# One-core S5 scan and dilated attention: wider products, two copied key rows, a shorter weighted sum, and powers and reloads on ScalarE

## The chip, the cores and the metric

The kernel runs on one core of one Trainium2 chip. The time is the device time of one execution, as the median of several runs. TensorE (PE) multiplies matrices into PSUM, VectorE (DVE) and ScalarE (ACT) work on tiles of 128 partitions, GpSimd (POOL) makes constants and SyncE (SP) issues most of the transfers. Data that is too large for one tile step lives in SBUF; the results of matmuls lie in PSUM banks and have to be evicted by DVE or ACT before a bank is used again.

## The reference: what is computed

Two independent layers act on inputs of 2048 positions by 448 features, in bf16, and their outputs stand side by side.

```python
# A: a diagonal state-space layer, 448 complex states
Lam_bar = exp(dt * Lam);  B_bar = ((Lam_bar - 1) / Lam)[:, None] * Bmat
h[t] = Lam_bar * h[t-1] + (x @ B_bar.T)[t]
y = 2 * real(h @ Cmat.T) + x * Dskip
# B: dilated sliding attention, 16 heads of 28, 8 taps, step 2
logits[s, w] = q[s] . k[s - 2 w] * 28**-0.5      (masked where s - 2w < 0)
o[s] = sum_w softmax(logits)[s, w] * v[s - 2 w]
out = concat(y, o @ wo)
```

## The kernel before, in words

The 2048 positions are laid out as 128 columns (position blocks) of 16 rows j. So a shift by two positions is a shift by two rows of a tile, and only where it runs past the first row does it become a shift by one column.

**Layer B.** PE projects q and k into PSUM banks `qk_ps`; ACT (L215, L217) and DVE (L219, L221) evict them into the tile `qk`. For half of the queries at a time (b = 1, then b = 0), DVE multiplies q with k row by row for two of the eight taps in one instruction, into the tile `prods` (L651, L653, L657). Shifts that run past row 0 need other rows and a column offset, so such a product is cut into several instructions. A ring of three buffers of 4096 columns holds products. PE sums the products over the head's dimensions into `logits` (L669, L675), with 32 columns of the array per matmul, and adds the mask (L287). DVE takes the maximum (`mx`, L698), PE subtracts it, ACT takes the exponential (L708), PE sums, DVE normalizes (L717, L719) and SP transposes the result into `attn`. Meanwhile PE projects v into banks `v_ps` (L750 opens a bank, L757 fills it) and ACT evicts them into `vd`. The weighted sum is made four times, for four groups g of queries. In each, four multiplications of 3584 columns (L814) alternate with three additions (L817), and one addition of 1792 columns joins the halves (L826; in two parts for the last group, L829). The result is transposed and multiplied with `wo` (L864, L888, L895).

**Layer A.** The 448 states are seven blocks m. For each of them DVE makes the matrices of powers `pw` as one product of 128x1920 (L1177). Input terms are summed by PE into banks `scp`, `scb`, `scP` (L1227, L1236), and a chain of short matmuls with ACT evictions between them carries the state over the columns (L1246 to L1287). Sixteen times a state is put back into a bank by a matmul with the identity (L1303, L1317). `y_ps` collects the output with `Ccat`, and a part with `Dg` (made by ACT, L1132).

**What sets the order.** A list of unit numbers, `ORDER`, is run by a planner, which appends each unit's instructions to its engine. A unit that may go to ACT or DVE stands there with 1000 added for its second engine. Each engine then runs its own list in order, and a semaphore makes it wait for what another engine has to deliver. There are six banks `s` and one two-bank buffer `W` of PSUM. A `v_ps` matmul that opens a bank waits until ACT or DVE has evicted what was in it before.

Of the kernel before, what the change touches and what calls it, by code (L numbers as in the profile page):

```python
# [96 lines left out]
def vec2(n):  # L97
    return n / 1920.0 + 0.07
# [107 lines left out]
class Ctx:  # L206
# [111 lines left out]
class PartB:  # L318
# [262 lines left out]
    def qk(self, b, prio):  # L581
# [8 lines left out]
        for g in (2 * b + 1, 2 * b):  # L590
            par = g - 2 * b
            j0 = 4 * g
            for tp in (3, 2, 1, 0):
# [967 lines left out]
```

## Time and profile before

| | |
|---|---|
| median of 3 runs | 139.11 us (138.9 to 139.13) |
| profiled execution, span | 136.8 us |
| PE busy | 131.0 us (96%), 1066 matmuls |
| DVE busy | 123.1 us (90%), 134 instructions |
| ACT busy | 88.3 us (65%), 199 instructions |
| granted TensorE clock | 1.00 in all stretches |

The span is from the first to the last recorded instruction. The page gives the profiled execution no other time than that span; what the runs measure is 2.3 us more. A busy share counts instructions from start to end, and on one engine a next one can begin before the last has ended; so the distance from one start to the next is the price of an instruction in a row of them, and it is less than its duration.

### The profile page before, as it was taken

What the parts mean: (1) busy time and instruction counts of PE and PEld (TensorE: products, weight loads), DVE (VectorE), ACT (ScalarE), POOL (GpSimd) and SP (SyncE); (2) the same over time, 40 slices, a digit from 0 to 9 for tenths busy, and PEclk for the clock granted to TensorE, in tenths of its full rate; (3) what the DMA queues carried; (4) which work ended last, traced back from release to release, by engine and by line L of the source; (5) the groups of instructions that cost most, each with busy time, mean ns of one, the idle gap of its engine ahead of it and who ended that gap; (6) DMA issues with size and microseconds to landing.
All of it is one profiled execution on the core that took longest, in us unless ns stands there. A gap on an engine that the chain in (4) does not pass through costs nothing.

```text
span 136.8 us, 2838 instructions
## 1 busy us (share of the span) xinstructions
PE 131.0 (96%) x1066; PEld 67.2 (49%) x1071; DVE 123.1 (90%) x134; ACT 88.3 (65%) x199; POOL 17.5 (13%) x69
## 2 busy tenths in 40 slices
PE   7999999999999999999999999999999999999890
PEld 2534335444455453656444564556665545545450
DVE  1379998999999999997999999999999999999950
ACT  3455588998554976757795998779546461433561
POOL 7489830025000000000000000000000000000000
PEclk9999999999999999999999999999999999999999
DMA  4968943647555524667999029460074425744263
GB/s 130 271 128 204 187 87 59 156 117 112 84 113 53 99 50 108 172 119 113 195 218 203 0 41 233 133 143 3 0 61 109 138 65 146 160 136 134 74 194 101
DMA packets 41694, 16.58 MB, mean 121 GB/s; under 512 B 33685, under 2 KB 41044, under 8 KB 41681
## 3 DMA queue, kind: packets, MB, share of 16 engines
q1 hardware_dynamic: 41618, 16.40, 54.8%
q8 instruction: 8, 0.13, 0.4%
q14 instruction: 5, 0.04, 0.1%
q10 hardware_dynamic: 63, 0.01, 0.0%
HBM read 4.32 MB, written 3.67 MB: 58 GB/s over the span
## 4 chain that ended last, share of the span: by engine, by line
DVE 39%; PE 38%; SPq 10%; issue 5%; ACT 3%; DMA 2%; DVEq 0%; ACTq 0%
DVE rb L817 12%; DVE prods L814 11%; SPq L363 7%; PE v_ps L757 6%; PE scb L1227 5%; DVE rb L814 4%; PE scp L1227 4%; PE logits L669 3%; DVE pw L1177 2%; DMA rb<-in_B_x_dram 2%; PE qk_ps L478 2%; DVE prods L653 2%; PE wo_ps L895 2%; DVE rb L826 2%; ACT qk L215 1%
## 5 line engine op out<-in xcount | busy, mean ns | idle before, releaser
L814 DVE TENSOR_TENSOR prods<-attn,vd 128x3584 bf16<-128x3584 bf16 x12 | 24.0, 2016 | 0.0
L817 DVE TENSOR_TENSOR rb<-rb,prods 128x3584 bf16<-128x3584 bf16 x11 | 22.2, 2018 | 0.1
L653 DVE TENSOR_TENSOR prods<-qk 128x3072 bf16<-128x3072 bf16 (+1 forms) x15 | 19.1, 1324 | 0.0
L215 ACT CAST qk<-wo_ps 128x448 bf16<-128x448 f32 (+1 forms) x16 | 8.2, 527 | 10.0 <-PE wo_ps L888 7.8
L478 PE MATMUL qk_ps<-rb 128*128 128x512 bf16 x60 | 14.4, 379 | 0.3 <-DMA rb<-in_B_x_dram 0.3
L1424 PE MATMUL y_ps<-Ccat,qk 128*128 128x448 bf16 x60 | 14.6, 352 | 0.0
L215 ACT CAST vd<-v_ps 128x448 bf16<-128x448 f32 x16 | 7.9, 540 | 5.2 <-PE v_ps L757 4.9
L1227 PEld LDWEIGHTS <-Bcat 128*128 128x128 bf16 x84 | 7.5, 100 | 7.4 <-issue 1.1
L1274 ACT CAST ubuf<-scb 128x64 bf16<-128x64 f32 x35 | 7.3, 220 | 5.9 <-PE scb L1281 3.5
L1424 PE MATMUL y_ps<-Ccat,h 128*128 128x448 bf16 x45 | 11.0, 353 | 0.0
L1227 PE MATMUL scb<-xaT_sb,Bcat 128*128 128x512 bf16 x42 | 10.9, 380 | 0.0
L757 PE MATMUL v_ps<-rb 128*128 128x448 bf16 x48 | 10.1, 353 | 0.0
L217 ACT ACTIVATE qk<-qk_ps 64x512 bf16<-64x512 f32 (+1 forms) x15 | 8.9, 599 | 1.5 <-PE qk_ps L485 1.0
L478 PEld LDWEIGHTS <-rb 128*128 128x128 bf16 x60 | 5.6, 97 | 7.4 <-issue 0.7
L657 DVE TENSOR_TENSOR prods<-qk 128x768 bf16<-128x768 bf16 (+3 forms) x18 | 9.1, 565 | 0.1
L1424 PEld LDWEIGHTS <-qk 128*128 128x128 bf16 x60 | 5.9, 98 | 5.4
L814 DVE TENSOR_TENSOR rb<-attn,vd 128x3584 bf16<-128x3584 bf16 x4 | 8.1, 2020 | 0.1
L888 PE MATMUL wo_ps<-wo_p,rb 128*128 128x448 bf16 x36 | 8.1, 353 | 0.0
L1177 DVE TENSOR_TENSOR pw<-Dm,spair 128x1920 bf16<-128x1920 bf16 x7 | 8.0, 1150 | 0.0
L1227 PE MATMUL scp<-xaT_sb,Bcat 128*128 128x512 bf16 x30 | 7.8, 381 | 0.0
L215 ACT CAST qk<-qk_ps 128x512 bf16<-128x512 f32 (+2 forms) x11 | 6.3, 585 | 2.3 <-PE qk_ps L485 1.1
L215 ACT CAST qk<-y_ps 128x448 bf16<-128x448 f32 (+1 forms) x9 | 5.6, 662 | 3.1 <-PE y_ps L1424 3.1
(197 smaller groups left out, 258.9 us busy)
## 6 DMA issues: line engine op xcount, KB each, us to landing
out_dram<-qk SPq DMA_DIRECT2D x32, 112.0 KB, 1.7
vd<-vd SPq DMA_DIRECT2D x3, 392.0 KB, 4.4
rb<-in_B_wqkv_dram SPq DMA_DIRECT2D x3, 336.0 KB, 4.4
qk<-in_A_x_dram SPq DMA_DIRECT2D x1, 448.0 KB
ra<-in_A_B_re_dram SPq DMA_DIRECT2D x1, 392.0 KB, 4.2
ra<-in_A_B_im_dram SPq DMA_DIRECT2D x1, 392.0 KB
rb<-in_A_C_re_dram SPq DMA_DIRECT2D x4, 98.0 KB, 2.9
rb<-in_A_C_im_dram SPq DMA_DIRECT2D x4, 98.0 KB, 3.9
```

Source lines behind the costliest of these rows:

```text
L215: nc.scalar.copy(out, in_)
L217: nc.scalar.mul(out, in_, scale)
L363: nc.sync.dma_start(self.xT[:, j], bass.AP(x.tensor, x.offset + j * D - DT, [[T * D, NCH], [1, KT * NCH]]), transpose=True)
L478: nc.tensor.matmul(out(n), lhsT=w(n, full, k), rhs=self.xT[:, j:j + 4, k, :], start=(not rfirst and k == 1), stop=(rfirst and k == KT - 1) ...
L653: V.tensor_tensor(out.rearrange("p i j k q -> p i (j k) q"), qq.unsqueeze(1).to_broadcast([NCH, 2, 4 * nk, NCH]), bass.AP(kk.tensor, kk.of ...
L657: V.tensor_tensor(jk(out[:, i, a:e]), qq, kk, op=ALU.mult)
L757: nc.tensor.matmul(box["ps"][:].rearrange("p h d -> p (h d)"), lhsT=self.xT[:, j, k, :], rhs=self.wv[:, k, :], start=False, stop=(k == KT ...
L814: V.tensor_tensor(tmp[i].rearrange("p (j d h) -> p j d h", j=8, d=DH), aa, self.vd[:, o:o + 8], op=ALU.mult)
L817: V.tensor_tensor(acc, acc, tmp[i], op=ALU.add)
L1177: V.tensor_tensor(t[:], self.o["Dm"][:].rearrange("p (a b) -> p a b", b=2).unsqueeze(1).to_broadcast([NCH, 2 * NPW, 32, 2]), self.sp[:, m ...
L1227: mt(box[i], lhsT=self.Bcat[:, k, m, :], rhs=self.xk(slice(i, None, 4), k), start=(i % 2 == 0 and k == 0), stop=False, **kw)
L1424: nc.tensor.matmul(ps, lhsT=h, rhs=self.Ccat[:, m, :], start=(m == 0 and not skip), stop=(m == NM - 1), skip_group_check=True)
```

## The change

1. **Products of up to four taps.** Two rows are kept ahead of row 0 in the key tiles, copies of the last two rows shifted by one column (`u_halo`, `u_halo3`). Products of q and k are cut by half of the taps and no longer by two: 6144 columns where four taps have one form, 3072 or 1536 otherwise. The products of the remaining 64 feature rows have their own buffer of 2048 columns, and the ring has two buffers of 6144. The sums on PE take 512 columns a matmul, not 256.
2. **Weighted sum.** The eight products of a group lie side by side in the space of the ring: two multiplications of 3584 columns and one of 7168, then one addition of 7168, one of 3584 and one of 1792 columns (the last group: two parts of the last).
3. **Powers on ACT.** A unit `powers` may go to ACT: 30 instructions of 64 columns with a scale from a tile of 128 x 1. `ORDER` sends one of the seven there (1257). One more POOL instruction makes the scale tile.
4. **Reloads on ACT.** A state that is put back into a bank can be a copy by ACT. `ORDER` sends five of the sixteen there.
5. **A new `ORDER`** for all units; some setup tiles are used again in place.

The core of the diff:

```diff
+        self.u_halo = cx.double(768, self.kTh[:, 0:KH, :, 2:QW], self.kT[:, T - KH:T, :, 0:NCH], [self.u_pad[1], *self.u_k[3]], 0)
+        self.u_halo3 = cx.double(256, self.k3h[:, 0:KH, 2:QW], self.k3[:, T - KH:T, 0:NCH], [...], 0)
...
+                        out = ub["pr"][:, p0:p0 + np_].rearrange("p i j k q -> p i (j k) q")
+                        qq = jk(q[:, j0:j0 + 4]).unsqueeze(1).to_broadcast([NCH, np_, 4 * nk, NCH])
+                        kk = jk(kh[:, KH + o:KH + o + 4, :, c:c + NCH])
+                        V.tensor_tensor(out, qq, bass.AP(kk.tensor, kk.offset, [kk.ap[0], [DIL * nk * QW, np_], *kk.ap[1:]]), op=ALU.mult)
...
+                            nc.tensor.matmul(at(h, i), lhsT=z, rhs=pr[:, :, i, k, :].rearrange("p (a b) q -> p a b q", a=2),
...
-                    def add(i):
-                        V.tensor_tensor(acc, acc, tmp[i], op=ALU.add)
...
+            def fold(n, out=None, pb=pb):
+                V.tensor_tensor(pb[:, 0:n] if out is None else out, pb[:, 0:n], pb[:, n:2 * n], op=ALU.add)
...
+            for u0, nu in ((5, 1), (4, 1), (0, 2)):
...
+            if eng == "ACT":
+                for k in range(NPW):
+                    for h in range(2):
+                        nc.scalar.activation(t[:, 2 * k + h].rearrange("p a b -> p (a b)"), self.o["Dm"][:], ACT.Copy,
+                                             scale=self.sp32[:, h, m * NPW + k:m * NPW + k + 1])
...
+            def reload(eng, out, in_):
+                if eng == "ACT":
+                    nc.scalar.copy(out, in_)
+                else:
+                    mt(out, lhsT=cx.ident[:], rhs=in_, start=True, stop=False, **kw)
...
+    0, 4, 21, 22, 2, 3, 1, 5, 6, 37, 39, 38, 24, 41, 9, 26, 42, 1040, 28, 29, 50, 8, 51, 45, 1043, 63, 46, 30, 7,
...
+    136, 494, 188, 182, 1257, 186, 138, 485, 495, 507, 143, 512, 513, 515, 131, 180, 514, 144, 524, 508, 516, 510,
```

Three places show how the instructions move. The first is ACT between the last evictions of q and k (`qk_ps`) and the exponential of the softmax of b = 1 (`ex_sb`). Before:

```order
L217 ACTIVATE qk<-qk_ps 64x512
L217 ACTIVATE qk<-qk_ps 128x4x128 x2
L215 CAST vd<-v_ps 128x448 x12
L215 COPY xaT_sb<-xaT_sb 64x4x128
L215 CAST vd<-v_ps 128x448 x2
L708 ACT_TABLE_LOAD
```

In the changed kernel:

```order
L220 ACTIVATE qk<-qk_ps 128x4x128 x3
L218 CAST vd<-v_ps 128x448 x2
L1157 ACTIVATE pw<-Dm,sh 128x64 x30
L218 CAST vd<-v_ps 128x448 x6
L218 COPY xaT_sb<-xaT_sb 64x4x128
L218 CAST vd<-v_ps 128x448
L218 COPY qk<-qk 128x2x128
L218 CAST vd<-v_ps 128x448 x3
L686 ACT_TABLE_LOAD
```

The 30 instructions of one block of powers now stand between the second and the third eviction of `v_ps`; the copy of `qk` is the smaller of the two copied pairs of key rows.

The second place is PE just ahead of the mask of b = 1 (the matmuls from `mrow` and `mcol`). Before:

```order
L750 MATMUL v_ps_756<-rb_70 128x448 [waits Activation_49]
L750 LDWEIGHTS rb_70
L750 MATMUL v_ps_757<-rb_70 128x448 [waits Activation_49]
L287 LDWEIGHTS mcol_130 [waits Pool_49]
L287 MATMUL logits_388<-mrow_129,mcol_130 128x4
```

In the changed kernel:

```order
L728 MATMUL v_ps_679<-rb_70 128x448 [waits Activation_49]
L728 LDWEIGHTS rb_70
L728 MATMUL v_ps_680<-rb_70 128x448 [waits Activation_49]
L735 LDWEIGHTS rb_70
L735 MATMUL v_ps_679<-rb_70 128x448
L735 LDWEIGHTS rb_70
L735 MATMUL v_ps_679<-rb_70 128x448
L735 LDWEIGHTS rb_70
L735 MATMUL v_ps_679<-rb_70 128x448
L290 LDWEIGHTS mcol_130 [waits Pool_49]
L290 MATMUL logits_476<-mrow_129,mcol_130 128x4
```

In both, six matmuls that open `v_ps` banks (the last two are shown) wait for ACT ahead of the mask. In the changed kernel three matmuls that fill the fifth bank stand between as well, and the six evictions that they wait for are the six behind the 30 instructions above.

The third place is DVE ahead of the maximum of b = 1. Before:

```order
L657 TENSOR_TENSOR prods<-qk 128x1536
L653 TENSOR_TENSOR prods<-qk 128x1024
L653 TENSOR_TENSOR prods<-qk 128x3072 x2
L653 TENSOR_TENSOR prods<-qk 128x1024
L653 TENSOR_TENSOR prods<-qk 128x3072
L653 TENSOR_TENSOR prods<-qk 128x1024
L698 TENSOR_REDUCE mx<-logits 128x128
L653 TENSOR_TENSOR prods<-qk 128x3072 x2
L657 TENSOR_TENSOR prods<-qk 128x256 x2
```

In the changed kernel:

```order
L645 TENSOR_TENSOR prods<-qk 128x6144
L578 COPY qk<-qk 128x24
L645 TENSOR_TENSOR prods<-qk 128x2048
L645 TENSOR_TENSOR prods<-qk 128x6144
L676 TENSOR_REDUCE mx<-logits 128x128
L645 TENSOR_TENSOR prods<-qk 128x6144
L645 TENSOR_TENSOR prods<-qk 128x2048
L695 RECIPROCAL rsum<-sm_ps 128x128
```

The products ahead of the maximum are fewer and larger (ten with 34,816 columns, before 21 with 32,768), and between the maximum and the reciprocal there are two products, where there were twelve and one of the powers.

More of the change, by code (lines that the diff above doesn't have):

```diff
@@ L293, in warm @@
         nc, P = self.nc, self.plan
-        self.pr = self.pool.tile([NCH, 3 * 4096], bf16, name="prods")
-        self.pr_ring = Ring(3)
-        self.pr_ring.get()
+        self.pr = self.pool.tile([NCH, 2 * QKM + QKR], bf16, name="prods")
+        self.pr_ring = Ring(2)
         z = nc.const_aps.tensor(1.0, [NCH, 512], bf16)
@@ L588, in qk, with pieces @@
         begun = set()
-        first = True
+        done = {}
+        def pieces(j0, hf, cut):
+            res = []
+            for p in range(4):
+                w = 3 - p + 4 * hf
+                o = j0 - DIL * w
+                o, c = (o, 2) if o >= -KH else (o + T, 0)
+                if res and p not in cut and res[-1][3] == c and res[-1][2] + DIL * res[-1][1] == o:
+                    res[-1][1] += 1
+                else:
+                    res.append([p, 1, o, c])
+            return res
         for g in (2 * b + 1, 2 * b):
@@ L667, in summ @@
-                    for kt in range(3):
+                    at = lambda h, i: lg[32 * i:32 * i + 32, 4 - 4 * h:8 - 4 * h, :].rearrange("p (b a) q -> p a b q", b=2)
+                    new = not rest and hf not in begun
+                    begun.add(hf)
+                    for h, z, k in ((0, cx.Z[:, 3, zs], 0), (1, cx.Zh[:, zs], 0)) if rest else [(hf, cx.Z[:, k, zs], k) for k in range(3)]:
                         for i in range(4):
-                            nc.tensor.matmul(at(tp, i),
-                                             lhsT=cx.Z[:, kt, zs], rhs=pr[:, :, i, kt, :],
-                                             start=(new and kt == 0), stop=(kt == 2), skip_group_check=True)
@@ L672, in summ @@
-                    if tp < 2:
-                        for z, t2 in ((cx.Z[:, 3, zs], tp + 2), (cx.Zh[:, zs], tp)):
-                            for i in range(4):
-                                nc.tensor.matmul(at(t2, i),
-                                                 lhsT=z, rhs=ub["p3"][:, :, i, 0, :],
-                                                 start=False, stop=True, skip_group_check=True)
-                    cx.pr_ring.put(ub["r"])
-                if split:
-                    near = [*self.u_q[b, par], *(x for j in range(j0, j0 + 4) for x in self.u_k[(j - DIL * ws[1]) // 4])]
-                    u = P.add("DVE", vec2(1536), lambda f=prod: f(only=0), near, prio, acq="PR")
-                    prods.append(u)
-                    u = P.add("DVE", vec2(1536), lambda f=prod: f(only=1), [*deps, u], prio)
-                else:
-                    u = P.add("DVE", sum(vec2(x[0]) for x in ops()), prod, deps, prio + (g % 2 == 0) * 0.1, acq="PR")
@@ L686, in qk @@
-                prods.append(u)
-                u = P.add("PE", 0.33 if tp > 1 else 0.55, summ, [u] + sums[:1], -2, rel="PR", acq="W" if first else None, mode="c")
+                            nc.tensor.matmul(at(h, i), lhsT=z, rhs=pr[:, :, i, k, :].rearrange("p (a b) q -> p a b q", a=2),
+                                             start=(new and k == 0), stop=(rest or k == 2), skip_group_check=True)
+                    if not rest:
+                        cx.pr_ring.put(ub["r"])
+                prods += units
@@ L688, in qk @@
+                dd = units + sums[:1] + ([done[2 * b + 1, 0], done[2 * b + 1, 1]] if rest else [])
+                u = done[g, hf] = P.add("PE", pe(2 if rest else 3, 512), summ, dd, -2, rel="P3" if rest else "PR",
+                                        acq=None if sums else "W", mode="c")
                 sums.append(u)
-                first = False
         self.u_prod[b], self.u_lg[b] = prods, sums
@@ L838, in pv, with mul @@
-            lasts[r] = [last, last]
-            if 2 * b + r == 0:
-                last = P.add("DVE", cost, lambda: step(part=1), [last], prio - 0.1 * r)
-                lasts[r][1] = last
-            self.pv_last = last
-            if not hasattr(self, "u_first"):
-                self.u_first = last
+            g = 2 * b + r
+            pb = cx.pr[:, 0:8 * n1]
+            def mul(u0, nu, r=r, g=g, pb=pb):
+                o, w0 = 4 * g + DIL * u0, 4 * (u0 // 4) + 2 * (u0 % 2)
+                v = self.vd[:, o:o + 8]
+                aa = self.attn[b][:, w0:w0 + 2 * nu, :, r, :].rearrange("q y i h -> q (y i) h").unsqueeze(2).to_broadcast(
+                    [NCH, 8 * nu, DH, H])
+                vv = bass.AP(v.tensor, v.offset, [v.ap[0], [DIL * D, nu], *v.ap[1:]])
+                V.tensor_tensor(pb[:, w0 * n1:(w0 + 2 * nu) * n1].rearrange("p (u j d h) -> p u j d h", u=nu, j=8, d=DH),
+                                aa.rearrange("q (u j) d h -> q u j d h", u=nu), vv, op=ALU.mult)
@@ new lines, in pv @@
+            last = first = P.add("DVE", vec2(4 * n1), lambda f=fold: f(4 * n1), muls, prio - 0.1 * r, mode="r")
+            if g > 0:
+                last = P.add("DVE", vec2(2 * n1), lambda f=fold: f(2 * n1), [last], prio - 0.1 * r, mode="r")
+                last = P.add("DVE", vec2(n1), acc, [last], prio - 0.1 * r, mode="r")
+                lasts[r] = [last, last]
+            else:
+                last = P.add("DVE", vec2(n1), lambda f=half: f(0), [last], prio - 0.1 * r, mode="r")
+                lasts[r] = [last, P.add("DVE", vec2(n1), lambda f=half: f(1), [last], prio - 0.1 * r)]
@@ L845, in pv @@
+            self.pv_dep = [first], [lasts[r][1]]
         for r in (1, 0):
```

254 lines of the change are left out of this document (108 added, 146 removed), and 61 rows, old and new, of the table ORDER.

## The prediction, made before the changed kernel was run

> **What bounds the kernel now.** I read the page first.
>
> ```profile
> span 136.8 us, 2838 instructions
> PE 131.0 (96%) x1066; PEld 67.2 (49%) x1071; DVE 123.1 (90%) x134; ACT 88.3 (65%) x199; POOL 17.5 (13%) x69
> DVE 39%; PE 38%; SPq 10%; issue 5%; ACT 3%; DMA 2%; DVEq 0%; ACTq 0%
> ```
>
> PE and DVE share the chain that ends last almost evenly, and ACT holds 3% of it. The sums below are made against this span of 136.8 us; the median, 139.11, is 2.3 us more, and I add the same 2.3 to each forecast. The busy time by stage shows whether one of the two is slack somewhere. Columns are the stretch, its length, and busy time and count on PE, weight loads, DVE, ACT and POOL.
>
> ```profile
> 34.00:44.00 10.00, 10.00 (x120) 4.97 (x119) 9.83 (x13) 5.04 (x12) 0.00 (x0) 1.00 0.54 85
> 44.00:54.00 10.00, 9.86 (x95) 4.53 (x93) 10.00 (x11) 7.65 (x13) 0.00 (x0) 1.00 0.38 83
> 64.00:96.00 32.00, 31.70 (x227) 16.50 (x227) 31.83 (x21) 26.39 (x77) 0.00 (x0) 1.00 0.60 129
> 96.00:128.00 32.00, 32.00 (x220) 17.35 (x218) 31.76 (x19) 14.05 (x28) 0.00 (x0) 1.00 0.44 109
> ```
>
> Neither is. From 34 us to 128 us both engines have work nearly all the time, at the full granted clock (1.00). So a saving on DVE alone shortens the span only as far as PE follows, and a stall that hits both is added to the span. ACT is the one with room: 5.04 of 10 us in the stretch from 34 to 44. Its timeline there, and two rows of later work that I need for prices:
>
> ```profile
> 33.96 0.54 ACT L215 CAST vd<-v_ps 128x448 bf16<-128x448 f32 x1
> 36.12 2.28 ACT L215 CAST vd<-v_ps 128x448 bf16<-128x448 f32 x5 [1.61 <-PE v_ps L757]
> 39.68 1.10 ACT L215 CAST vd<-v_ps 128x448 bf16<-128x448 f32 x2 [1.29 <-PE v_ps L757]
> 41.38 0.97 ACT L215 CAST vd<-v_ps 128x448 bf16<-128x448 f32 x2 [0.60 <-PE v_ps L757]
> 43.77 1.10 ACT L215 CAST vd<-v_ps 128x448 bf16<-128x448 f32 x2 [1.42 <-PE v_ps L757]
> 46.75 1.28 ACT L708 ACT_TABLE_LOAD   x1
> 48.05 1.02 ACT L708 ACTIVATE ex_sb<-logits 128x1024 bf16<-128x1024 f32 x1
> ...
> 81.59 1.30 ACT L1132 ACTIVATE Dg<-ident,dsk 128x128 bf16<-128x128 bf16 x4
> ...
> 88.21 0.33 ACT L1274 CAST ubuf<-scb 128x64 bf16<-128x64 f32 x2
> ```
>
> ACT waits there four times for `v_ps`, 4.9 us in all; five evictions in a row take 2.28 us, so one every (2.28 - 0.54) / 4 = 0.435.
>
> ```profile
> 42.27 0.74 PE L750 MATMUL v_ps<-rb 64*128 64x448 bf16 x6
> 42.94 0.20 PE L287 MATMUL logits<-mrow,mcol 128*128 128x4 bf16 x2
> 46.57 1.46 PE L1227 MATMUL scp<-xaT_sb,Bcat 128*128 128x512 bf16 x6
> 49.17 0.84 PE L669 MATMUL logits<-prods,Zsel 128*32 128x256 bf16 x24
> 49.84 0.28 PE L675 MATMUL logits<-prods,Zsel 128*32 128x256 bf16 x4
> ...
> 130.00 1.05 PE L864 MATMUL pt_o<-ident,rb 128*128 128x128 bf16 x16 [0.43 <-DVE qk L1436]
> 130.88 2.43 PE L895 MATMUL wo_ps<-wo_p,rb 128*128 128x448 bf16 x12
> ```
>
> On PE the six matmuls that open `v_ps` banks run without a stall, the mask follows at 42.94, and only at 130.00 does PE wait 0.43 for DVE; its last matmul ends at 133.3. DVE:
>
> ```profile
> 15.43 0.68 DVE L221 TENSOR_SCALAR qk<-qk_ps 128x512 bf16<-128x512 f32 x1
> 16.03 0.67 DVE L219 CAST qk<-qk_ps 128x512 bf16<-128x512 f32 x1
> ...
> 19.74 1.15 DVE L1177 TENSOR_TENSOR pw<-Dm,spair 128x1920 bf16<-128x1920 bf16 x1
> 20.81 0.62 DVE L1125 TENSOR_TENSOR Gd<-Dm,gs 128x896 bf16<-128x896 bf16 x1
> ...
> 43.73 1.22 DVE L698 TENSOR_REDUCE mx<-logits 128x128 bf16<-128x1024 f32 x1
> ...
> 63.05 1.23 DVE L698 TENSOR_REDUCE mx<-logits 128x128 bf16<-128x1024 f32 x1 [0.80 <-PE logits L287]
> ...
> 116.23 3.95 DVE L814 TENSOR_TENSOR prods<-attn,vd 128x3584 bf16<-128x3584 bf16 x2
> ...
> 126.02 2.09 DVE L829 TENSOR_TENSOR rb<-rb,prods 128x1792 bf16<-128x1792 bf16 x2
> 128.03 1.08 DVE L1401 TENSOR_TENSOR qk<-qk,rb 128x1792 bf16<-128x1792 bf16 x1
> 129.32 2.15 DVE L1436 TENSOR_TENSOR qk<-y_ps,qk 128x448 bf16<-128x448 f32 x3 [0.20 <-DVE qk L1401]
> ```
>
> The mask is there before DVE needs it at 43.73; the last half of the weighted sum ends at 126.02 + 2.09 = 128.11, and 5.2 us of tail follow on PE.
>
> **The change part by part. DVE's prices.** Two groups give the price of an instruction beside its columns:
>
> ```profile
> L814 DVE TENSOR_TENSOR prods<-attn,vd 128x3584 bf16<-128x3584 bf16 x12 | 24.0, 2016 | 0.0
> L653 DVE TENSOR_TENSOR prods<-qk 128x1024 bf16<-128x1024 bf16 x6 | 4.1, 684 | 0.0
> ```
>
> A column costs (2016 - 684) / 2560 = 0.52 ns, and 151 ns remain for the instruction. In a row less is paid: the pair at 116.23 starts 3.95 - 2.02 = 1.93 us apart, of which 1.865 is columns, so a merged instruction saves 0.07 to 0.08 us, and at most 0.15. Merging is therefore cheap to value. Products: 37 to 17 instructions for the same 57,344 columns, 20 x 0.07 = 1.4 us. Weighted sum: 32 to 24, 0.6 us. The block of powers that leaves, from one start to the next: 20.81 - 19.74 = 1.07. Two evictions fewer at 16.03 - 15.43 = 0.6: 1.2. The multiplication of the skip (L1401, 1.0) and one addition of `y_ps` (0.6: the three at 129.32 take 2.15 us for four times 448 columns, and a single one pays its own start) move ahead of the last half, so they no longer lie in the tail. To the last half DVE has 1.4 + 0.6 + 1.07 + 1.2 - 1.6 = 2.7 us less to do. No price here is far from a row, except for a multiplication of 6144 or 7168 columns with four taps on overlapping rows: between the columns' price and the same with 0.15 us more for each of 17 such instructions, 2.5 us against the change. I take the columns' price, since products of two taps with the same form of operand cost it now.
>
> **PE's prices.** Matmuls of 512 columns start (1.46 - 0.38) / 5 = 0.216 us apart, so five reloads that leave save 1.08. The sums of products: 24 of 256 columns, four side by side, take 49.84 - 49.17 = 0.67, or 0.112 for four where 256 columns stream in 0.108; so twice the columns in half the matmuls saves next to nothing (0.2 in all). In columns, PE has 127.0 us to do instead of 128.1, and what stands from the mask of b = 1 to the end is the same within 0.15 us, since one pair of `v_ps` banks (8 x 0.19) moved behind it. The copied rows and the reloads are put on ACT (0.5 to 0.7 us each), which the windows show with 2 to 5 us free in each 10; without that cover the five reloads would put 2.5 us into the chain of the state.
>
> **The powers on ACT** are the term that decides. Thirty ACTIVATEs of 64 columns with a scale for each partition. The trace has no such instruction. Its nearest rows from below are the 64-column casts of L1274: two start 0.33 - 0.22 = 0.11 apart, without that scale. From above there are four of L1132, with a scale for each partition at 128 columns: the last ends 1.30 after the first starts, at 0.42 each, so one every (1.30 - 0.42) / 3 = 0.29. Thirty make 3.3 us by the one and 8.8 by the other. L1132 has the form of operands, so I take it less 64 columns at ACT's price (0.435 for 448 columns against 0.11 for 64: 0.85 ns a column), 0.24 each, 7.2 us.
> The Trainium skill (ScalarE: Activation LUTs, "What ACT_TABLE_LOAD costs") speaks against the low price: an operand of one value per partition adds about 93 ns to 186 + 0.833 N, and neighbours overlap by 93. By it an instruction here would be an estimated 0.24 us; its figure at 128 columns, 0.293, agrees with L1132 (0.29).
>
> What is queued behind. The order on ACT is two evictions of `v_ps`, the block, six more. ACT reaches the first of the two at about 33.96, as now; the block runs from 34.8 to 42.0, and the six evictions end 0.435 apart, the last at 44.65. On PE, the six matmuls that open `v_ps` banks wait for these six, and behind them stand three that fill a bank (0.56) and the mask. So the mask comes at 44.65 + 0.19 + 0.56 = 45.4, not 42.94: PE stands still for about 2.5 us, and DVE's maximum, for which DVE would be free at 41.7 (fewer instructions) to 43.7 (if key rows are as late as now), starts at 45.5, 1.8 late.
>
> The queues:
>
> ```profile
> L724 SPq DMA_TRANSPOSE attn<-attn_t x2: 1275/1553/1831, 58.7 to 89.4; - x2
> DMA to landing us min/median/max: 3.3/3.4/3.5
> ...
> L403 SPq DMA_DIRECT2D wo_p<-in_B_wo_dram x8: 337/422/424, 50.4 to 53.6; - x8
> ```
>
> On SP the eight loads of `wo_p` (8 x 0.42 = 3.4 us) and the four pairs of transfers inside `vd` now stand behind the transposition of b = 1, which waits for the normalization. The first product that reads those rows of `vd` is the third of the weighted sum, behind some 10 us of DVE work from the normalization on (four products' groups, powers, maximum) and two multiplications (3.9). So I cost it at nothing, and at up to 3.4 us were that work not there. POOL's one more instruction stands ahead of its work on `vd`, and the powers need its tile only at 34.8; nothing as well.
>
> From there two sums. DVE: after the maximum it has 2048 columns (1.07) and 9 products' starts (0.65) less, 0.6 from the weighted sum, 1.6 more from the two pieces that moved ahead, and the wait of 0.80 at 63.05 is covered by a block of powers that now stands ahead of it: -1.5. Against it the normalization waits for ACT's exponential, which is behind those evictions, about 0.4. The tail without those two pieces is 0.3 shorter. End: +1.8 - 1.5 + 0.4 - 0.3 = **+0.4**. PE: +2.4 at the mask, the same work behind it, 0.15 less, and the wait of 0.43 at the end gone: **+1.8**. PE's 86.9 us of columns behind the mask take 133.3 - 42.9 = 90.4 now, so up to 3.5 us are gaps, some of which a late PE may lose. I take the middle: +1.1, **140.2 us**; this case alone lies between 139.2 and 141.2.
>
> **Rivals.**
> *The block is short or its cover holds* (other side: faster). Everything hangs on the distance of the 30 ACTIVATEs. At 0.11 the block ends at 38.1, the six evictions at 40.7, the mask is at 41.5, and ACT's 4.9 us of waiting have paid for all of it. DVE then gains 2.0 to the maximum and up to 1.5 behind, PE 1.4 at the mask and 0.15 behind. PE bounds it: -1.5, **137.6 us** (136.6 to 138.4). It decides below about 0.16 per instruction, or if PE's or DVE's products are themselves so late that nothing waits at 42. For it: the casts at 0.11, and ACT's idle time. Against it: L1132.
> *The late mask is made up in the gaps.* DVE's +0.4 and a PE that loses 1.8 of its 3.5 us of gaps: the two effects cancel, **139.1 us**. For it: the new order can fill waits of the state's chain. Against it: PE was busy 31.70 of 32 us there, so the gaps are pieces of a few hundredths.
> *The wide operands or the reloads cost more.* 2.5 us more on DVE as bounded above, or ACT's reloads in the state's chain, on top of the block: **142 us**. Against it: L653's two-tap form already runs at the columns' price.
>
> **How the numbers follow.** Forecast 0.46, block hidden 0.34, made up 0.12, costlier 0.08. A time within 0.2% (0.28 us) can't be told from no change. Faster: 0.32 from the hidden block and 0.02 from the third: 0.34. Same: 0.02, 0.09 and 0.02 from the forecast: 0.13. Slower: the rest, 0.53. Cases of both signs hold most of the chance; the range 136.9 to 141.4 takes in the forecast's own and most of the hidden block's, and leaves out 0.2: the costlier case and the ends.
>
> **What would show it.** In the changed profile: L1157 x30 with its busy stretch on ACT, 7.2 us or 3.3; the rows L728 on PE with a wait for ACT ahead of L290; DVE's L676 with a wait for PE of about 2 us near 43 to 45; the end of L793 near 128.8, and PE's last matmul at 133.7 to 135.1. L645 at 6144 columns should take 3.35 us and L785 at 7168 3.88. A block of 7 us without a wait at L676 would refute the chain, not the price; the last matmul ahead of 132.5 refutes the forecast.

## The result, and the profile after

The changed kernel is slower: 143.97 us (142.96 to 144.23, four runs) against 139.12 for the kernel before, a ratio of 1.0338 with a 95% interval of 1.0301 to 1.0375. The direction was forecast; the time lies outside the range of 136.9 to 141.4. Two executions of kernels further below ran at a much lower granted clock (170.59 us at 0.76, 156.56 us at 0.856) and are left out of their medians. Three lines of the page of the changed kernel:

```profile
span 142.0 us, 2580 instructions
PE 134.1 (94%) x938; PEld 64.3 (45%) x938; DVE 119.6 (84%) x102; ACT 99.1 (70%) x237; POOL 17.5 (12%) x70
DVE 44%; PE 35%; ACT 9%; issue 5%; DMA 3%; SPq 2%; DVEq 0%; ACTq 0%
```

DVE has 3.5 us less to do than before, and the span is 5.2 us longer. ACT's share of the chain of waits has gone from 3% to 9%. Where that lies, the timeline of ACT shows (start, length, engine, line and operation, output and inputs, count; in brackets the idle time ahead and what ended it):

```profile
34.45 0.97 ACT L218 CAST vd<-v_ps 128x448 bf16<-128x448 f32 x2 [0.56 <-PE v_ps L735]
35.30 7.27 ACT L1157 ACTIVATE pw<-Dm,sh 128x64 bf16<-128x64 bf16 x30
42.47 2.65 ACT L218 CAST vd<-v_ps 128x448 bf16<-128x448 f32 x6
```

The block of powers takes 7.27 us, and the six evictions behind it end at 45.12. PE (timeline; the last three rows are the tail):

```profile
41.43 0.39 PE L659 MATMUL logits<-prods,Zhi 128*32 128x512 bf16 x4
43.03 2.66 PE L728 MATMUL v_ps<-rb 64*128 64x448 bf16 x6 [1.22 <-ACT vd L218]
45.63 1.30 PE L735 MATMUL v_ps<-rb 128*128 128x448 bf16 x3
46.72 0.24 PE L290 MATMUL logits<-mrow,mcol 128*128 128x4 bf16 x2
46.82 2.58 PE L735 MATMUL v_ps<-rb 128*128 128x448 bf16 x9
...
128.87 1.49 PE L1415 MATMUL y_ps<-Ccat,S 128*128 128x448 bf16 x7 [0.62 <-DVE qk L1427]
133.28 1.50 PE L837 MATMUL pt_o<-ident,prods 128*128 128x128 bf16 x24
136.14 2.43 PE L868 MATMUL wo_ps<-wo_p,rb 128*128 128x448 bf16 x12
```

PE stands still from 41.8 to 43.0, then opens six banks one eviction apart, and the mask comes at 46.72. The last matmul ends at 138.57, where it ended at 133.31. And in the busy time by stretches of one microsecond the third-last number, PE's granted clock (it stands behind the busy times and counts of PE, weight loads, DVE, ACT and POOL), shows what no row of the kernel before did:

```profile
42.00:43.00 1.00, 0.00 (x0) 0.00 (x0) 1.00 (x1) 1.00 (x5) 0.00 (x0) 1.00 0.61 106
44.00:45.00 1.00, 0.84 (x3) 0.19 (x2) 0.00 (x0) 1.00 (x3) 0.00 (x0) 0.94 0.50 104
45.00:46.00 1.00, 0.99 (x4) 0.15 (x3) 0.00 (x0) 0.73 (x2) 0.00 (x0) 0.50 0.68 126
46.00:47.00 1.00, 1.00 (x6) 0.49 (x5) 0.00 (x0) 0.03 (x1) 0.00 (x0) 0.50 0.49 98
48.00:49.00 1.00, 1.00 (x6) 0.46 (x5) 1.00 (x2) 0.66 (x2) 0.00 (x0) 0.85 0.63 131
```

From 44.9 to 48.3 us the clock is 0.50 (the means of 0.94 and 0.85 give the two ends). DVE:

```profile
16.38 0.69 DVE L222 CAST qk<-qk_ps 64x504 bf16<-64x504 f32 x1 [1.05 <-ACT qk L218]
...
28.76 1.23 DVE L645 TENSOR_TENSOR prods<-qk 128x2048 bf16<-128x2048 bf16 x1 [0.42 <-ACT qk L218]
...
30.61 8.30 DVE L645 TENSOR_TENSOR prods<-qk 128x6144 bf16<-128x6144 bf16 x3 [0.40 <-ACT qk L218]
...
39.04 4.49 DVE L645 TENSOR_TENSOR prods<-qk 128x2048 bf16<-128x2048 bf16 x2
47.01 1.23 DVE L676 TENSOR_REDUCE mx<-logits 128x128 bf16<-128x1024 f32 x1 [3.49 <-PE logits L290]
...
53.39 0.96 DVE L695 RECIPROCAL rsum<-sm_ps 128x128 f32<-128x128 f32 x1 [0.76 <-PE sm_ps L691]
...
124.39 3.89 DVE L789 TENSOR_TENSOR prods<-prods 128x7168 bf16<-128x7168 bf16 x1
128.19 0.62 DVE L1427 TENSOR_TENSOR qk<-y_ps,qk 128x448 bf16<-128x448 f32 x1
128.73 2.08 DVE L793 TENSOR_TENSOR prods<-prods 128x1792 bf16<-128x1792 bf16 x2
```

DVE is free for the maximum at 39.04 + 4.49 = 43.53 and waits 3.49 us for the mask. The last half of the weighted sum ends at 130.81, 2.70 later than before; and behind it PE needs 7.76 us to its end, where it needed 5.20.

### The profile page after: what moved, and what is told of

Same layout as the page of the kernel before. It is cut to its first block, busy times and chain, and to the rows that moved or that the text cites. A ratio compares the mean times of both kernels' runs of the same rounds, so it can differ in the third digit from the quotient of the medians.

```text
span 142.0 us, 2580 instructions
## 1 busy us (share of the span) xinstructions
PE 134.1 (94%) x938; PEld 64.3 (45%) x938; DVE 119.6 (84%) x102; ACT 99.1 (70%) x237; POOL 17.5 (12%) x70
## 4 chain that ended last, share of the span: by engine, by line
DVE 44%; PE 35%; ACT 9%; issue 5%; DMA 3%; SPq 2%; DVEq 0%; ACTq 0%
DVE prods L785 22%; DVE prods L789 13%; PE qk_ps L482 7%; PE v_ps L735 5%; ACT pw L1157 5%; PE logits L659 3%; PE y_ps L1415 3%; DMA rb<-in_B_wqkv_dram 3%; PE qk_ps L515 3%; DVE rb L789 2%; DVE pw L1160 2%; ACT vd L218 2%; PE wo_ps L868 2%; PE scb L1210 2%; PE scp L1210 2%
## 5 line engine op out<-in xcount | busy, mean ns | idle before, releaser
L645 DVE TENSOR_TENSOR prods<-qk 128x3072 bf16<-128x3072 bf16 (+4 forms) x17 | 31.7, 1910 | 0.9 <-ACT qk L218 0.8
L785 DVE TENSOR_TENSOR prods<-attn,vd 128x3584 bf16<-128x3584 bf16 (+1 forms) x12 | 31.2, 2641 | 0.1
L789 DVE TENSOR_TENSOR prods<-prods 128x7168 bf16<-128x7168 bf16 (+1 forms) x7 | 21.6, 3089 | 0.1
L482 PE MATMUL qk_ps<-rb 128*128 128x512 bf16 x60 | 14.9, 379 | 0.4 <-DMA rb<-in_B_wqkv_dram 0.3
L735 PE MATMUL v_ps<-rb 128*128 128x448 bf16 x48 | 11.7, 386 | 0.0
L220 ACT ACTIVATE qk<-qk_ps 128x512 bf16<-128x512 f32 (+1 forms) x15 | 8.6, 596 | 2.0 <-DVE qk L222 1.1
L482 PEld LDWEIGHTS <-rb 128*128 128x128 bf16 x60 | 5.4, 98 | 7.4 <-issue 1.4
L218 ACT CAST qk<-qk_ps 128x512 bf16<-128x512 f32 (+1 forms) x14 | 8.2, 585 | 0.4
L659 PE MATMUL logits<-prods,Zsel 128*32 128x512 bf16 x112 | 7.3, 381 | 0.1
L735 PEld LDWEIGHTS <-rb 128*128 128x128 bf16 x48 | 4.4, 104 | 6.4 <-issue 3.5
L1157 ACT ACTIVATE pw<-Dm,sh 128x64 bf16<-128x64 bf16 x30 | 7.3, 339 | 0.0
```

The lines of the kernel that those rows point to most:

```text
L218: nc.scalar.copy(out, in_)
L220: nc.scalar.mul(out, in_, scale)
L482: nc.tensor.matmul(out(n), lhsT=w(n, full, k), rhs=self.xT[:, j:j + 4, k, :], start=(not rfirst and k == 1), stop=(rfirst and k == KT - 1) ...
L645: V.tensor_tensor(out, qq, bass.AP(kk.tensor, kk.offset, [kk.ap[0], [DIL * nk * QW, np_], *kk.ap[1:]]), op=ALU.mult)
L659: nc.tensor.matmul(at(h, i), lhsT=z, rhs=pr[:, :, i, k, :].rearrange("p (a b) q -> p a b q", a=2), start=(new and k == 0), stop=(rest or k ...
L735: nc.tensor.matmul(box["ps"][:].rearrange("p h d -> p (h d)"), lhsT=self.xT[:, j, k, :], rhs=self.wv[:, k, :], start=False, stop=(k == KT ...
```

## The experiments

All ratios are to the kernel before, measured beside it on the same chip (138.82 to 139.12 us). Three things had to be told apart: what the block on ACT costs by its waits, what the low clock adds, and why the rest of the change brings nothing.

| kernel | us | ratio (95%) |
|---|---|---|
| changed kernel | 143.97 | 1.0338 (1.0301 to 1.0375) |
| changed, powers back on DVE | 140.90 | 1.0138 (1.0109 to 1.0167) |
| changed, half of the block on ACT | 140.03 | 1.0081 (1.0056 to 1.0107) |
| changed, PE filled, ten matmuls | 143.51 | 1.0339 (1.0306 to 1.0372) |
| changed, PE filled once, five matmuls | 142.39 | 1.0253 (1.0227 to 1.0279) |
| before, with the block alone | 147.67 | 1.0605 (1.0540 to 1.0670) |
| half block, reloads on PE | 140.03 | 1.0080 (1.0065 to 1.0096) |
| half block, output row 13 earlier | 139.67 | 1.0058 (1.0037 to 1.0078) |
| half block, 1.07 us more on DVE, late | 140.99 | 1.0153 (1.0134 to 1.0172) |
| half block, 1.07 us more on DVE, early | 140.40 | 1.0114 (1.0089 to 1.0138) |
| before, 1.07 us more on DVE, late | 140.23 | 1.0093 (1.0078 to 1.0108) |
| before, 1.07 us more on DVE, early | 139.74 | 1.0059 (1.0038 to 1.0080) |
| before, weighted sum of the change alone | 138.52 | 0.9972 (0.9957 to 0.9986) |
| before, three blocks of powers on POOL | 148.25 | 1.0694 (1.0654 to 1.0733) |
| before, both of the last two | 148.96 | 1.0713 (1.0682 to 1.0744) |

### The block on ACT

The whole block back on DVE:

```diff
-    136, 494, 188, 182, 1257, 186, 138, 485, 495, 507, 143, 512, 513, 515, 131, 180, 514, 144, 524, 508, 516, 510,
+    136, 494, 188, 182, 257, 186, 138, 485, 495, 507, 143, 512, 513, 515, 131, 180, 514, 144, 524, 508, 516, 510,
```

> The changed kernel with one number of the order altered: the block of powers that went to ACT is made by DVE again (one product of 128x1920, at the same place of the list). Theory 1 (the 7.3 us block on ACT holds up six evictions, so PE stands still, its mask comes at 46.7 instead of about 43, and PE's lateness is carried to the end, with the lower granted clock after the standstill on top): mask near 43.5, the maximum on DVE near 44.6 (DVE has 1.07 us more ahead of it), clock 1.00, span 137.5 to 138.5, time 139.7 to 140.7. Theory 2 (the time is lost in the wide products, the weighted sum and the new order, and the block only shows where DVE and PE would have waited anyway): at most 1 us faster, 143 to 144. If the block alone explains all and the rest of the change brings what its DVE sum says: about 137.5.

Measured 140.90, just above theory 1's range.

Half of the block on ACT (16 of the 30), the rest on DVE:

```diff
             if eng == "ACT":
-                for k in range(NPW):
+                n1 = 8
+                V.tensor_tensor(t[:, 2 * n1:], ..., op=ALU.mult)
+                for k in range(n1):
                     for h in range(2):
```

> The changed kernel with the block on ACT cut to 16 instructions; DVE makes the other 14 pieces as one product of 128x896 (0.54 us) at the same place of the list. Theory 1: the block takes 3.9 us and ends near 39.2, its six evictions near 41.9, before PE's sums of products for b = 1 are done (41.8), so the mask comes near 42.8 and the time is that of the kernel with the powers on DVE within 0.5 us, 139.4 to 140.5; ACT's price for one instruction stays 0.24. Theory 2: 143 to 144. A step, not a proportion, is what theory 1 asks for: half of the block takes away nearly all of the loss.

Measured 140.03. Half of the block takes away 1.0338 - 1.0081 = 2.6%, or 3.6 us, and taking the other half away as well gains nothing more: with the whole block back on DVE the time is 0.57% longer again (1.0138 against 1.0081). In its timeline of ACT:

```profile
36.25 3.93 ACT L1163 ACTIVATE pw<-Dm,sh 128x64 bf16<-128x64 bf16 x16
40.08 2.81 ACT L218 CAST vd<-v_ps 128x448 bf16<-128x448 f32 x6
```

In its timeline of PE, at the same place and in the tail:

```profile
42.69 0.74 PE L728 MATMUL v_ps<-rb 64*128 64x448 bf16 x6
43.95 0.19 PE L290 MATMUL logits<-mrow,mcol 128*128 128x4 bf16 x2
...
125.69 1.48 PE L1421 MATMUL y_ps<-Ccat,S 128*128 128x448 bf16 x7 [0.62 <-DVE qk L1433]
132.96 2.43 PE L868 MATMUL wo_ps<-wo_p,rb 128*128 128x448 bf16 x12
```

And in its timeline of DVE, the maximum and the end of the last half:

```profile
44.80 1.22 DVE L676 TENSOR_REDUCE mx<-logits 128x128 bf16<-128x1024 f32 x1
...
125.55 2.08 DVE L793 TENSOR_TENSOR prods<-prods 128x1792 bf16<-128x1792 bf16 x2
```

The block ends at 40.2, the evictions at 42.89, the six matmuls that open banks run without a stall, and DVE doesn't wait at its maximum. It is the step that theory 1 asked for, between a block that is covered and one that stops PE: 3.93 us are covered, 7.27 are not; where between them the threshold lies was not measured.

The same block, alone, in the kernel before (its number in `ORDER` also moves back, to behind the second eviction of v, and POOL makes the tile of scales):

```diff
+            if m == 1:
+                for k in range(NPW):
+                    for h in range(2):
+                        nc.scalar.activation(t[:, 2 * k + h]..., self.o["Dm"][:], ACT.Copy, scale=self.sp32[...])
...
-        u = P.add("DVE", vec2(2 * NPW * PL), build, [self.u_s, *deps], prio, acq="pw")
+        u = P.add("ACT" if m == 1 else "DVE", vec2(2 * NPW * PL), build, [self.u_s, *deps], prio, acq="pw")
```

> The kernel before with one part of the change alone: the second block of powers goes from DVE to ACT as the same 30 instructions, behind the second eviction of v, and POOL makes their scale tile. Theory 1: ACT makes the block from about 36.5 to 43.8, where it had 4.9 us of waits; the evictions behind it are some 5 us late, PE stands still for 3 to 4 us ahead of the mask, its clock falls, DVE has 1.07 us less: 142 to 144.5. Theory 2 (the block's place is covered by ACT's waits, and other parts of the change cost the time): 138 to 139.5.

Measured 147.67, more than theory 1 asked for. Here the block stands ahead of the evictions on which two banks wait much earlier (timeline of PE):

```profile
44.88 0.96 PE L750 MATMUL v_ps<-rb 64*128 64x448 bf16 x2 [5.49 <-ACT vd L215]
45.77 4.66 PE L757 MATMUL v_ps<-rb 128*128 128x448 bf16 x12
```

Two stretches of it in the busy time by stretches:

```profile
44.00:46.00 2.00, 1.12 (x3) 0.23 (x3) 0.31 (x1) 2.00 (x6) 0.00 (x0) 0.57 0.47 85
50.00:52.00 2.00, 2.00 (x38) 1.13 (x38) 0.00 (x0) 0.97 (x2) 0.00 (x0) 0.72 0.32 77
```

PE stands still for 5.49 us; and then twelve matmuls that take 2.44 us in the kernel before take 4.66, at a clock of 0.50 (by the means of 0.57 and 0.72, from 44.3 to 51.1).

### The clock

Matmuls of zeros on PE, added to the logits bank, ahead of the matmuls that open banks (five ahead of the first, one ahead of each other; in the second kernel only the five):

```diff
...
+                zc, oc = cx.zero[:], nc.const_aps.tensor(1.0, [NCH, 512], bf16)
                 for j, rows, box in pair:
+                    for _ in range({10: 5, 11: 1, 7: 1, 6: 1, 1: 1, 0: 1}.get(j, 0)):
+                        nc.tensor.matmul(self.lg[1][:, 0:4, :], lhsT=zc, rhs=oc, start=False, stop=True, skip_group_check=True)
```

> The changed kernel with ten matmuls of zeros (0.216 us each, 512 columns, added to the logits bank, which they leave as it is) on PE just where it stands still: five ahead of the first of the six matmuls that open banks of v, one ahead of each of the others. The block on ACT and all waits stay. Theory of the clock (PE's near standstill from 41.8 to 45.1 is what brings the granted clock to 0.50 for about 3.5 us): clock 1.00 throughout, mask near 46.0, time 0.8 to 1.6 lower, 142.3 to 143.1, as in the one run of the changed kernel whose clock was 1.00 (142.96). Rival (the clock falls for another reason): clock near 0.985 again and 143.7 to 144.3. In both, DVE still waits some 3 us at its maximum.

The clock was 1.00 in the profile, as expected, and the time was not lower: 143.51, ratio 1.0339. The ones in between had a price of their own: a bank was opened every 0.61 us, not every 0.44, so the mask was no earlier.

> The changed kernel with five matmuls of zeros ahead of the first of the six matmuls that open banks of v, and none between these (with one ahead of each, the six came 0.61 us apart instead of 0.44, so the mask was as late as without them though the clock stayed at 1.00). If the clock needs only that PE does not stand quite still for 1.2 us: clock 1.00, the six 0.44 apart, mask 0.8 us earlier, 142.6 to 143.1. If the thin work after it (0.19 of each 0.44 us) is what lowers the clock: clock near 0.985, 143.7 to 144.3.

A stretch of the second kernel, and its timeline of PE (the last row is its last matmuls):

```profile
45.00:46.00 1.00, 0.92 (x5) 0.31 (x4) 0.00 (x0) 0.80 (x2) 0.00 (x0) 1.00 0.39 79
```

```profile
43.10 2.48 PE L733 MATMUL v_ps<-rb 64*128 64x448 bf16 x6
45.51 0.74 PE L740 MATMUL v_ps<-rb 128*128 128x448 bf16 x3
46.09 0.19 PE L292 MATMUL logits<-mrow,mcol 128*128 128x4 bf16 x2
46.14 1.86 PE L740 MATMUL v_ps<-rb 128*128 128x448 bf16 x9
...
134.74 2.43 PE L873 MATMUL wo_ps<-wo_p,rb 128*128 128x448 bf16 x12
```

Measured 142.39, clock 1.00. Three matmuls that fill a bank take 0.74 instead of 1.30, nine 1.86 instead of 2.58. So the low clock is worth 1.0338 - 1.0253 = 0.85%, 1.2 us of the 4.7 (0.6 to 1.8 by the two intervals taken together); from here to the kernel with half of the block, 1.0253 - 1.0081 = 1.7% or 2.4 us, is the wait itself.

### What is left: 1.1 us with half of the block

Six kernels tell where the saved work of DVE went. First the reloads, back on PE (`1247`, `1286`, `1325`, `1402`, `1403` in the order without their 1000):

> The kernel with half of the block on ACT (140.03, 1.0081 of the kernel before), with the five reloads of a state back on PE as matmuls with the identity. Theory 1a (behind the mask PE sets the end, and ACT's reloads make PE wait in the chain of the state: its gaps there are 2 us longer than before, the longest of them ahead of matmuls that wait for ACT's eA and ubuf): PE gets 1.08 us more work but loses less of it to waits: 139.5 to 140.1. Theory 1b (the reloads on ACT are as good as PE's 1.08 us saved): 140.6 to 141.2.

Measured 140.03, the same as with them on ACT (1.0080 and 1.0081). Theory 1b is out. Of 1a the time fits, by a trade: PE no longer waits for DVE in the tail, and does 1.08 us more.

One unit of PE moved ahead of the wait in the tail:

```diff
-    ... 684, 616, 674, 686, 582, 685, 609, 583, 585, 679, 687, ...
+    ... 684, 616, 674, 679, 686, 582, 685, 609, 583, 585, 687, ...
```

> The kernel with half of the block on ACT, with one unit of PE moved: the matmuls of the output row 13 (seven, 1.3 us, which wait for nothing) now stand ahead of those of row 15, ahead of which PE stands still for 0.62 to 0.79 us at 125 us, until DVE has done a long addition of 7168 columns and the addition that frees the bank. Theory 1 (PE sets the end and this standstill is carried to it): 0.6 to 0.8 us less, 139.2 to 139.5. Rival (DVE sets the end): within 0.2 us of 140.03.

Measured 139.67: 0.2% (0.3 us) less than with half of the block, about half of what theory 1 asked for, and the intervals overlap, so the gain isn't clear of noise. The wait is gone from the trace, but PE had less to gain than its length.

1.07 us more on DVE, by making a block of powers twice; late, in the weighted sum, and early, ahead of the maximum; in both kernels:

```diff
+              for _ in range(2 if m == 5 else 1):     # early: m == 0
                 V.tensor_tensor(
```

> The kernel with half of the block on ACT, with one product of the powers made twice by DVE near 82 us (1.07 us more on DVE, in the weighted sum). If PE sets the end and DVE has come free of it: 140.0 to 140.4. If DVE sets the end, or PE waits for it in the tail (the bank that frees PE at 125 us is freed by DVE): 140.8 to 141.2.

> The kernel before, with the same product made twice by DVE near 85 us (1.07 us more on DVE). The prediction treated DVE and PE as two bounds that both end last, DVE by its chain to the last half: then 139.6 to 140.1. If PE alone sets the end before: 138.8 to 139.2.

> The kernel with half of the block on ACT (140.03, 1.0081 of the kernel before), with the first product of the powers made twice by DVE near 22 us, ahead of the maximum of b = 1 (the same 1.07 us that cost 0.96 when they stood in the weighted sum). Theory (ahead of the maximum DVE waits for key rows that PE and ACT deliver, so the work that the change saves there is lost to waits): at most 0.4 us more, 139.9 to 140.5. Rival (DVE's work sets the time of the maximum): 1 us more, 140.8 to 141.2.

> The kernel before, with its first product of the powers made twice near 21 us. DVE waits there 0.54 us behind it, and is otherwise busy to the maximum: 0.5 to 1.1 us more than before, 139.4 to 140.1. If key rows set the time of the maximum here too: within 0.3 us of before.

Late, the 1.07 us (1.19 in their place in these traces: the two products start 2.26 us ahead of what follows, where one starts 1.07 ahead) cost 0.72% (1.0 us) in the kernel with half of the block and 0.93% (1.3 us) in the kernel before. So DVE's work counts in full in both, though PE too has little rest, and PE alone doesn't set the end of the changed kernel. In the kernel with half of the block and the late 1.07 us, PE's timeline has in the tail, where the wait was 0.62:

```profile
126.30 1.48 PE L1422 MATMUL y_ps<-Ccat,S 128*128 128x448 bf16 x7 [1.07 <-DVE qk L1434]
```

Early, they cost 0.33% (0.46 us, within the noise of 0.35%) in the one and 0.59% (0.82 us) in the other; the difference of the two isn't clear of noise, so here the traces have to decide. DVE's timeline, in the kernel with half of the block and the early 1.07 us:

```profile
29.64 1.23 DVE L645 TENSOR_TENSOR prods<-qk 128x2048 bf16<-128x2048 bf16 x1
...
31.32 8.29 DVE L645 TENSOR_TENSOR prods<-qk 128x6144 bf16<-128x6144 bf16 x3 [0.24 <-ACT qk L218]
...
44.56 1.21 DVE L676 TENSOR_REDUCE mx<-logits 128x128 bf16<-128x1024 f32 x1
```

The waits of 0.42 and 0.40 for ACT's evictions of key rows have shrunk to none and 0.24, so about half of the extra work went where the waits had been. The other half reached the maximum: it is 38.39 us behind the first projection matmul (44.56 - 6.17), where it was 37.69 (44.80 - 7.11). In the kernel before nearly all of it did: 38.59 (44.87 - 6.28) against 37.54 (43.73 - 6.19). So DVE has some slack there in the changed kernel, about 0.5 us behind the first of its waits, and next to none before. Behind the last of these waits there is none either: the whole block back on DVE puts 0.5 us more there than half of it, and cost 0.57%.

### Parts that might help the kernel before

The weighted sum of the change, alone:

```diff
+                    if n == 0:
+                        mul(5, 1)
+                        mul(4, 1)
+                    elif n == 1:
+                        mul(0, 2)
+                    elif n == 2:
+                        V.tensor_tensor(pb[:, 0:4 * n1], pb[:, 0:4 * n1], pb[:, 4 * n1:8 * n1], op=ALU.add)
```

> The kernel before with the weighted sum of the change alone: two multiplications of 3584 columns, one of 7168, then additions of 7168, 3584 and 1792, in the old order. DVE has one start less in each of the four sums than the two multiplications and two additions that it replaces, 8 x 0.07 = 0.6 us. If DVE sets the end (1.07 us more on it cost 1.3): 138.1 to 138.5. If PE does, or if the wide additions hold back what waits behind them on DVE (a row of 3.9 us in which no bank is freed): 138.9 or more.

Measured 138.52, 0.9972 (0.9957 to 0.9986): 0.4 us faster than the kernel before, at the edge of the first range. In the tail nothing else has moved: in its DVE timeline the last half ends at 127.84, where it ended at 128.11.

```profile
125.75 2.09 DVE L830 TENSOR_TENSOR rb<-prods 128x1792 bf16<-128x1792 bf16 x2
```

Three blocks of powers on POOL, alone and with the weighted sum (their numbers also move forward in `ORDER`):

```diff
-            V.tensor_tensor(t[:], self.o["Dm"]...
+            (nc.gpsimd if m in (4, 5, 6) else V).tensor_tensor(t[:], self.o["Dm"]...
```

> The kernel before with the last three blocks of powers on POOL, which has nothing to do from 34 us on, and its four clears of vd ahead of them; DVE loses 3.2 us of work between 66 and 86 us. Theory (DVE and PE both end last, and PE has 0.4 to 0.6 us of wait for DVE in the tail): 0.4 to 1.2 us faster, 137.7 to 138.5. Rival (POOL slows DVE while both work on the same memory, or its block comes too late for the chain of the state): 139 or more, with DVE's products longer than 2.02 us while POOL is busy.

> Both of the last two together: DVE has 3.8 us less. If PE sets the end as soon as DVE has some 1 us less to do: as the better of the two, within 0.3 us. If DVE still sets it: the sum of both gains.

Measured 148.25 and 148.96. The rival holds, and far beyond its number (timeline of POOL in the first of the two, then of DVE, then of PE):

```profile
64.89 4.67 POOL L1177 TENSOR_TENSOR pw<-Dm,spair 128x1920 bf16<-128x1920 bf16 x1 [32.12 <-DVE mx L698]
70.67 4.03 POOL L1177 TENSOR_TENSOR pw<-Dm,spair 128x1920 bf16<-128x1920 bf16 x1 [1.12 <-PE scp L1323]
80.82 4.83 POOL L1177 TENSOR_TENSOR pw<-Dm,spair 128x1920 bf16<-128x1920 bf16 x1 [6.12 <-PE scP L1323]
```

```profile
66.21 10.37 DVE L814 TENSOR_TENSOR prods<-attn,vd 128x3584 bf16<-128x3584 bf16 x2
80.37 7.16 DVE L817 TENSOR_TENSOR rb<-rb,prods 128x3584 bf16<-128x3584 bf16 x2
```

```profile
88.78 1.01 PE L1317 MATMUL scp<-h,ident 128*128 128x512 bf16 x2 [8.04 <-DVE dsk L1046]
```

Two multiplications that take 3.95 us take 10.37 while POOL works, and two additions that take 4.08 take 7.16. PE then stands still for 8.04 us behind DVE, and its granted clock is 0.50 from 85.5 to 92.3, so what this kernel loses is not DVE's loss alone.

## Why the prediction was wrong, point by point

**The block's price: right.** 0.24 us for each instruction was taken, 7.2 in all; it was 7.27, and 3.93 for 16. The estimate from the Trainium skill (ScalarE: Activation LUTs, "What ACT_TABLE_LOAD costs"), 0.24, agrees.

**What queues behind it: right in place, short in size.** Predicted were 45.4 for the mask and 45.5 for the maximum; measured 46.72 and 47.01. The first eviction of v was at 34.45 instead of the 33.96 that I carried over, which is 0.5. The rest, 0.9, is mostly the clock: from the last eviction (45.12) to the mask the sum had 0.75, and it took 1.60; in the kernel filled once, with the clock at 1.00, it took 0.91 (46.09 - 45.18). The wait itself costs 2.4 us, measured as the step from the kernel filled once to half of the block; my two cases, 140.2 and 137.6, lay 2.6 apart, though both were some 2 to 4 us too early.

**The clock: not in the prediction.** I read the granted clock as 1.00 in every stretch of the kernel before and took it as given, at a cost of nothing. A change that stops PE can lose it, and did: 1.2 us.

**The failed step: PE's sum from the mask to the end, and the clock.** The forecast's later chain was PE's: +2.4 at the mask, then 0.15 and 0.43 less behind it, +1.8, and then the middle between it and DVE's +0.4, so +1.1. By the profiles PE's last matmul ends 5.26 us later than before (138.57 against 133.31), 3.78 of it at the mask (46.72 against 42.94) and 1.48 behind it (91.85 us from the mask to the end, before 90.37). In the kernel filled once, with the clock at 1.00 and the first projection matmul at the same time (6.16 us, before 6.19), it is 3.15 at the mask and 0.71 behind it (137.17 - 46.09 = 91.08). So of the 4.2 us that the forecast was short by in the profiles, 1.4 is the clock, 1.3 the work behind the mask, which became 0.71 longer where 0.58 less was summed, 0.75 the mask, and 0.7 the choice of the middle. The points below say why nothing was gained behind the mask.

**The DVE sum ahead of the maximum: wrong.** In the forecast itself the late mask hides this term; the faster rival rests on it. I bounded DVE's time for the maximum by 41.7 (less work) and 43.7 (key rows as late as now), and in the faster rival took the gain of 2.0 in full. It was 43.53, the late end. In the kernel with half of the block, where nothing else holds it up, the maximum is at 44.80, with the first projection matmul of that profile at 7.11; before it is 43.73 with 6.19. So from that matmul to the maximum it takes 37.69 us where it took 37.54, and 0.53 of that is the half of the block that DVE makes here. In the changed kernel DVE is free for it after 37.36 (43.53 - 6.17), so 0.2 us were gained of 2.0. The busy time from DVE's first eviction of q and k to that point, before and changed, shows where the rest went:

```profile
9.33:43.73 34.40, 34.06 (x307) 15.77 (x305) 33.05 (x47) 24.13 (x47) 11.11 (x26) 1.00 0.66 120
9.41:43.53 34.12, 32.55 (x224) 13.22 (x221) 31.48 (x33) 31.76 (x76) 10.44 (x26) 1.00 0.59 117
```

DVE has 1.57 us less to do there (33.05 against 31.48), and 1.29 of it became waits, 2.64 us of idle time against 1.35: the 1.05, 0.42 and 0.40 in the rows of DVE above, all for evictions by ACT. The extra early work, which stands behind the first and longest of them, confirms this in part: about half of it went into the other two. (The trace of the kernel before counts 39 products, not the 37 of my sum; that is 0.15 us.)

**The DVE sum behind the maximum: right.** Predicted -1.5 up to the last half. From 44.80 to 127.63 it is 82.83 us with half of the block, where it was 84.38 (128.11 - 43.73): -1.55. In the changed kernel it is 83.80 (130.81 - 47.01), 0.58 less, mostly because the normalization waits 0.76 us for PE's `sm_ps` where I allowed 0.4 for the late exponential. The wide instructions cost the columns' price: 7168 columns took 3.89 us.

**The tail, -0.3: wrong in sign.** Behind the last half PE needs 7.76 us, not 5.2, with the block and with half of it (135.39 - 127.63). That is where the -1.55 is given back. My sum took PE's tail from the last half on. In the changed order PE's last wait for DVE (0.62) is for an addition that frees its bank, behind 3.89 us of folding and ahead of the last half, and from there PE has 9.70 us of matmuls to do without another wait (135.39 - 125.69); before, 3.31 stood behind its last wait (133.31 - 130.00). With 1.07 us more on DVE the last half and PE's end both come later, and the distance stays (136.01 - 128.24 = 7.77). With one unit moved that wait is gone, and the time is only 0.3 us less, which isn't clear of noise: by that trace PE's own work from the mask on (135.00 - 43.84 = 91.16 us, before 90.37) then sets the end. Beside that wait PE's longest waits behind the mask are for ACT in the chain of the state (0.29 us at 62.5, 0.21 at 68.6 with half of the block, where the kernel before has none over 0.16); the rest was not isolated and stays open.

**The choice of the middle: wrong.** With a DVE chain that ends at +0.4 and a PE chain at +1.8 I forecast +1.1, by hoping for gaps that a late PE would lose. The 3.5 us of gaps came from PE's columns; in the trace of the kernel before PE is busy 89.29 of the 90.37 us behind the mask, so at most 1.08 is idle, and 0.43 of it was in the sum already:

```profile
42.94:133.31 90.37, 89.29 (x727) 48.00 (x730) 87.34 (x68) 58.70 (x144) 0.00 (x0) 1.00 0.52 116
```

No run shows PE winning any: from the mask to the end it took longer. The later of two chains was the forecast to make. It would have been 140.9, still 3 us short.

**The rivals.** The hidden block was tried by halving it: it hides, as its condition said (it had a threshold of 0.16 us an instruction, or 4.8 us in all), and the time is 140.0 instead of 137.6, for want of the gain ahead of the maximum and of one on PE behind the mask. The late mask made up in PE's gaps is out: PE took longer behind the mask, not less. Costlier wide operands are out: 3.35 and 3.89 us were the columns' prices. Costlier reloads on ACT are out, since the kernel without them takes the same time (140.03).

## What to carry to other kernels

Work that one engine saves ahead of a wait for its inputs goes into that wait first: ask which row delivers the operands, and count the gain only as far as that row moves. Work that it saves behind it counts only as far as the other engine, which ends last beside it, can follow. An instruction list on a third engine is priced by the nearest row with the same form of operands, and its place by what waits behind it; half of it may be free where the whole is not. And where two chains both end last, the forecast is the later one, with the clock that a stopped PE may lose.

## What the runs showed of the hardware that was not expected

**A standstill of 1.2 us, followed by thin work, can halve PE's clock.** PE stood still from 41.8 to 43.0 and then had one 448-column matmul in each 0.44 us (0.20 each where nothing holds them: 2.43 for the last twelve); the clock was 0.50 from 44.9 to 48.3. With five matmuls in the standstill, and the same thin work behind them, it stayed at 1.00. After 5.5 us of standstill it was at 0.50 from 44.3 to 51.1. The low stretches of four traces lasted 3.4, 6.8, 6.8 (85.5 to 92.3, three blocks on POOL) and 10.2 us (83.6 to 93.8, with the weighted sum as well), each about a multiple of 3.4. In the changed kernel PE was busy again all the while (0.99 and 1.00 of the microseconds from 45 to 47), so a lost clock did not come back at once. The Trainium skill (TensorE: Matmul & The Clock Gate, "HAM oscillation — how this bites in real kernels") gives as its rule that there be no idle gap of PE longer than about 3.4 us. Here a gap a third as long, with thin work behind it, was enough. The same page of the Trainium skill ("A second HAM failure mode: psum-queue depth-cycling") tells of a kernel whose clock went down and up because PE was idle for short times between its groups of matmuls. That is nearer to what this trace shows. In one run of four of the changed kernel the clock stayed at 1.00 and the time was 142.96.

**POOL and DVE stop each other.** A product of 128x1920 took POOL 4.0 to 4.8 us, and DVE's products of two SBUF operands lost 10.37 - 3.95 = 6.4 us beside the first two and 7.16 - 4.08 = 3.1 us beside the third. Both of DVE's pairs end 1.88 us after POOL's instruction (76.58 - 74.70 and 87.53 - 85.65), about the length of one product, as if DVE had waited POOL's instruction out. The Trainium skill (GPSIMD Engine Reference, "1. Specifications") says that POOL and DVE share SBUF interfaces, with contention where a DVE instruction has two SBUF inputs. The runs agree, and give the price: three products on POOL, 13.5 us there, took 3.4 us of work from DVE (three of 1.15) and cost it 9.5, and with PE's standstill and low clock behind it the kernel became 9.3 us longer (148.25 against 138.99).
